# A recurrence joined over two batch elements, and one product in its plain form, in a DeltaNet and MLP-mixer kernel

## The chip, the core and the metric

The kernel runs on one core of a Trainium2 chip. The metric is the device time of one execution in microseconds (us), as the median of several runs of the same program. A core has five engines that run side by side, each with its own instruction stream: TensorE (PE in the profile) multiplies matrices into the accumulator memory PSUM, VectorE (DVE) and ScalarE (ACT) work elementwise and empty PSUM, GpSimd (POOL) works elementwise in SBUF, and SyncE (SP) issues the DMAs of this kernel. Engines wait for one another by semaphores.

## The reference

Four batch elements, eight heads, 768 rows in sequence, head dimension 48. A recurrence runs along the rows for each head, and its output is the input of a token and channel mixer:

```python
k_n = k / (np.linalg.norm(k, axis=-1, keepdims=True) + 1e-06)
state = np.zeros((B, H, D, D), dtype=np.float32)
for t in range(S):
    kt, vt, bt = (k_n[:, :, t], v[:, :, t], beta[:, :, t, None])
    y[:, :, t] = np.einsum('bhd,bhde->bhe', q[:, :, t], state)
    v_old = np.einsum('bhde,bhd->bhe', state, kt)
    state = state + bt[:, :, :, None] * np.einsum('bhd,bhe->bhde', kt, vt - v_old)
...
x = y.transpose(0, 2, 1, 3).reshape(B, S, H * D)      # 4 x 768 x 384
h = np.maximum(x.transpose(0, 2, 1) @ w_tok1, 0.0) @ w_tok2   # 768 -> 256 -> 768
u = x + h.transpose(0, 2, 1)
return u + np.maximum(u @ w_ch1, 0.0) @ w_ch2         # 384 -> 1536 -> 384
```

## The kernel before, in words

**Tiling of the recurrence.** The 768 rows of an element are cut into 6 *units* of 128 rows (24 units in all), and each unit into 2 chunks of 64 rows. A chunk is one *step* of the recurrence: 12 steps per element, 48 in all, one element after the other. The eight heads stand as 4 pairs; the two heads of a pair sit in the two halves of the 128 partitions, so that a matmul of one head uses a 64-row or 48-row part of TensorE's array.

**What a unit needs before its steps.** Job k loads k and q, p prepares them (norms, scaling, transposes), c and d form the products of the rows of a chunk among themselves (p_g, L453). A triangular matrix per chunk is inverted: t takes its parts out, i inverts several units at a time on VectorE (a *round*; the last two rounds hold units 18 to 21 and 22 to 23) after a passage through device memory (n_dram, then w_dram), f brings the parts back (gm<-w_dram), and h or j joins them with small matmuls (p_z, p_x). Job v loads v for a unit by four DMAs (L413) and scales it on POOL (L426) into a tile v_st, of which there are two buffers.

**One step** (recur, job r) is a chain through three engines:
- p_k: 8 matmuls of the state s_t with k (L862); then VectorE subtracts v, giving rest (L869)
- p_y and p_w: 16 matmuls of the state with q (L882) and of the inverse with rest (L886); then ACT copies p_w to w_t (L892)
- p_s and p_y: 16 matmuls of w_t (L900, L901); then VectorE subtracts p_s from the state (L909), and ACT puts p_y into xb by two instructions (L914). xb is the element's 768 x 384 array, the mixer's input.

**The mixer** of an element (job m) starts when its 12 steps are done. It multiplies xb with w_tok1 (p, L1060) and that with w_tok2 (p_h, L1073) and adds the result to xb (L1077). Then for three *pairs* of 128-row blocks: six transposes per pair (p_ut, L1083, copied to u_t at L1087), the first product with w_ch1 and a relu, and the second product with w_ch2 (p_o, L1162), added to xb (L1091) and stored (L1094). The second product always uses a form with 7 smaller products. The first has two forms, chosen by the constant FAST: elements below FAST (only element 0 here) take the plain one, p_c (L1140, relu at L1149); the others take a form with 15 smaller products, p_r (L1032), which needs sums of the input blocks (forms, L1001, on VectorE), sums of the weights (job s), and additions of its results (L1041 copies on ACT, L1044 additions on VectorE, relu at L1048). The buffer for weight sums, lent, first holds k and q of early units. Three PSUM banks serve the mixer, two the recurrence, two the preparation.

**What sets the order.** Every job is a Python generator that issues some instructions between two yields. A string `order` written out in the program says which job makes its next steps (`r24*5` is five pieces of step 24), so the interleaving on every engine is fixed by hand, with no scheduler. All DMAs stand in one queue on SP in the order of the string, and each also waits for the one eight before it. Elements' recurrence steps stand between the matmuls of the mixer of the element before. Element 3's mixer has nothing beside it.

Each fp32 matmul appears in the trace as two records, so that `x8` in the order of instructions is x16 in the trace.

## Time and profile before

| what | value |
|---|---|
| median of the runs | 639.9 us (639.62 to 640.89) |
| span of the profiled execution | 636.9 us |
| TensorE busy | 608.5 us (96%) |
| VectorE busy | 447.9 us (70%) |
| ScalarE busy | 268.0 us (42%) |
| GpSimd busy | 107.2 us (17%) |
| mean granted clock of TensorE | 0.976 |

The span runs from the first to the last instruction of one profiled execution. The time of a run also holds what lies around the span; by the median that is 3.0 us. Busy time is the union of an engine's instructions. Rows of the profile read: line and engine, operation, output<-inputs with shapes, count, busy time and mean duration in ns, then the engine's idle time just before these instructions and the instruction that ended it.

### The profile page before, as it was taken

How to read it: one execution, taken by the hardware profiler on the slowest of the kernel's cores; microseconds unless marked ns; L12 is line 12 of the kernel's file. 1: busy time of each engine (PE TensorE's matmuls, PEld its weight loads, DVE VectorE, ACT ScalarE, POOL GpSimd, SP SyncE). 2: the span in 40 equal slices, each digit the busy share in tenths (PEclk: the TensorE clock that was granted, in tenths of full speed). 3: DMA queues.
4: the chain of work that ended last, by engine and by line, in shares of the span. 5: the costliest groups of instructions: out<-in, count | busy, mean ns of one | idle time of the engine just before them, and what ended most of it. 6: DMA issues, size and time to landing. Idle time of an engine off the chain costs nothing.

```text
span 636.9 us, 21542 instructions
## 1 busy us (share of the span) xinstructions
PE 608.5 (96%) x9132; PEld 531.5 (83%) x9132; DVE 447.9 (70%) x1132; ACT 268.0 (42%) x693; POOL 107.2 (17%) x146
## 2 busy tenths in 40 slices
PE   8488988899999999999999999999999999999997
PEld 5367877668898988859889999769999987999997
DVE  4987876967999658988969987776728253373643
ACT  7758785447523342215624323325334130232240
POOL 2348354235210211111111001000010000000000
PEclk9978796999999999999999999999999999999999
DMA  9686666666543355344454223202020000000000
GB/s 201 127 148 151 153 142 153 162 135 162 110 113 89 71 116 101 76 109 79 90 103 95 43 82 58 48 5 42 5 53 2 27 2 0 26 1 26 2 26 26
DMA packets 135776, 50.27 MB, mean 79 GB/s; under 512 B 114656, under 2 KB 130144, under 8 KB 135680
## 3 DMA queue, kind: packets, MB, share of 16 engines
q1 hardware_dynamic: 135680, 48.89, 35.2%
q8 instruction: 72, 1.18, 0.8%
q14 instruction: 24, 0.20, 0.1%
HBM read 39.42 MB, written 9.44 MB: 77 GB/s over the span
## 4 chain that ended last, share of the span: by engine, by line
PE 82%; DVE 7%; ACT 4%; DMA 3%; issue 2%; POOL 1%; SPq 1%; ACTq 0%; DVEq 0%; POOLq 0%
PE p_o L1162 26%; PE p_r L1032 20%; PE p_c L1140 8%; PE p_h L1073 5%; PE p L1060 4%; PE p_k L862 3%; PE p_g L453 3%; PE p_y L882 3%; PE p_s L900 3%; PE p_w L886 1%; DVE sub L681 1%; DVE x L686 1%; PE p_y L901 1%; PE p_ut L1083 1%; PE p_z L785 1%
## 5 line engine op out<-in xcount | busy, mean ns | idle before, releaser
L1162 PE MATMUL p_o<-wc,r 128*128 128x192 f32 x720 | 126.1, 329 | 0.6 <-ACT u_t L1087 0.6
L1162 PEld LDWEIGHTS p_o<-wc,r 128*128 128x128 f32 x720 | 116.8, 190 | 2.7 <-ACT u_t L1087 1.1
L1044 DVE TENSOR_TENSOR r<-r,p_r 128x512 f32<-128x512 f32 x90 | 59.8, 684 | 38.1 <-PE p_r L1032 34.3
L1091 DVE TENSOR_TENSOR xb<-xb,p_o 128x192 f32<-128x192 f32 x84 | 29.3, 350 | 57.8 <-PE p_o L1162 57.3
L1041 ACT COPY r<-p_r 128x512 f32<-128x512 f32 x54 | 31.3, 585 | 85.7 <-PE p_r L1032 76.1
L686 DVE TENSOR_TENSOR x<-x,sub 128x84 f32<-128x84 f32 (+24 forms) x178 | 59.4, 334 | 6.1
L681 DVE TENSOR_TENSOR sub<-x 128x84 f32<-128x84 f32 (+24 forms) x178 | 58.0, 326 | 6.8 <-DMA x<-n_dram 2.3
L1162 PE MATMUL p_o<-wc,s 128*128 128x192 f32 x288 | 51.5, 331 | 0.3 <-DVE xb L1091 0.3
L1140 PE MATMUL p_c<-u_t,wc 128*128 128x256 f32 x216 | 51.0, 386 | 0.2 <-ACT u_t L1087 0.2
L1162 PEld LDWEIGHTS p_o<-wc,s 128*128 128x128 f32 x288 | 46.7, 190 | 1.4 <-DVE xb L1091 0.6
L1048 ACT ACTIVATE r<-r 128x512 f32<-128x512 f32 x54 | 34.0, 631 | 26.7 <-DVE r L1044 26.2
L426 POOL TENSOR_TENSOR v_st<-v_st,nrm 128x384 f32<-128x384 f32 x24 | 20.1, 838 | 146.3 <-DMA v_st<-in_v_dram 109.3
L1140 PEld LDWEIGHTS p_c<-u_t,wc 128*128 128x128 f32 x216 | 39.7, 190 | 6.0 <-ACT u_t L1087 0.4
L516 POOL TENSOR_TENSOR mb<-mask_c,cs 128x512 f32<-128x512 f32 x20 | 21.2, 1062 | 138.9 <-DVE cs L494 138.6
L914 ACT ACTIVATE xb<-p_y 64x192 f32<-64x192 f32 x96 | 31.2, 325 | 23.6 <-PE p_y L901 12.2
L892 ACT COPY w_t<-p_w 128x192 f32<-128x192 f32 x48 | 15.2, 316 | 58.0 <-PE p_w L886 57.5
L1032 PE MATMUL p_r<-u_t,wc 128*128 128x128 f32 x288 | 38.7, 277 | 0.0
L453 PE MATMUL p_g<-kq 48*64 48x128 f32 (+1 forms) x704 | 33.6, 281 | 3.8 <-ACT kq L529 3.3
L1032 PE MATMUL p_r<-t_d,wc 128*128 128x128 f32 x288 | 37.3, 280 | 0.0
L1032 PEld LDWEIGHTS p_r<-u_t,wc 128*128 128x128 f32 x288 | 35.3, 192 | 0.4
L1060 PE MATMUL p<-xb,w 128*128 128x384 f32 x96 | 34.9, 511 | 0.0
L1032 PEld LDWEIGHTS p_r<-t_d,wc 128*128 128x128 f32 x288 | 34.0, 192 | 0.8
(184 smaller groups left out, 1212.2 us busy)
## 6 DMA issues: line engine op xcount, KB each, us to landing
d<-in_moe_w_ch_dram SPq DMA_DIRECT2D x24, 384.0 KB, 3.5
v_st<-in_v_dram SPq DMA_DIRECT2D x96, 48.0 KB, 2.7
out_dram<-xb SPq DMA_DIRECT2D x23, 192.0 KB, 1.9
kst<-in_k_dram SPq DMA_DIRECT2D x64, 48.0 KB, 2.9
n_dram<-gm SPq DMA_DIRECT2D x72, 32.0 KB, 2.4
pads<-in_k_dram SPq DMA_DIRECT2D x24, 96.0 KB, 2.9
pads<-in_q_dram SPq DMA_DIRECT2D x24, 96.0 KB, 2.9
gm<-w_dram SPq DMA_DIRECT2D x72, 32.0 KB, 2.1
```

The source lines that it names most:

```text
L453: nc.tensor.matmul(p_g[PAR[i ^ cc], p], kqt[f, p, cc, 0], kqt[f, p, cc])
L681: nc.vector.tensor_tensor(out=tmp, in0=y[:, :, 0:s, s : s + 1].to_broadcast([n, k, s, w]), in1=y[:, :, s : s + 1, s + 1 : m].to_broadcast( ...
L686: nc.vector.tensor_tensor(out=y[:, :, 0:s, s + 1 : m], in0=y[:, :, 0:s, s + 1 : m], in1=tmp, op=ALU.add,)
L914: nc.scalar.mul(y[:, :, D * i : D * i + D], p_y[PAR[1 - i]], 1.0 if c else -1.0)
L1032: nc.tensor.matmul(p[:, i], pieces[i // width][:, at : at + 128], f[f"u{n}"], start=first and i == 0, stop=True, skip_group_check=True,)
L1041: nc.scalar.copy(o, p)
L1044: nc.vector.tensor_tensor(out=o, in0=o, in1=p, op=ALU.add if sign > 0 else ALU.subtract)
L1048: nc.scalar.activation(o, o, ACTF.Relu)
L1060: nc.tensor.matmul(p_1[dh], piece_of(w1, c, 0)[:, dh * 128 : (dh + 1) * 128], xb[:, c], start=(c == 0), stop=(c == NCH - 1),)
L1073: nc.tensor.matmul(p_h, piece_of(w2, j, c * 128)[:, c * 128 : (c + 1) * 128], r1[j], start=(j == 0), stop=(j == NDH - 1),)
L1140: nc.tensor.matmul(p_c[:, k], piece_of(wc1, cb, f * 128)[:, f * 128 : (f + 1) * 128], u_t[:, cb], start=(cb == 0), stop=(cb == NCB - 1),)
L1162: nc.tensor.matmul(p, a[:, m], wc2[:, m, j], start=(start and i == 0), stop=(i == NM - 1), skip_group_check=True,)
```

## The change

**One joint recurrence for elements 2 and 3.** Units 12 to 23 are numbered anew: even ones are chunks of element 2, odd ones the same chunks of element 3 (where). Steps 24 to 35 are 12 joint steps of 16 heads (recur_pair) in place of 24 steps of 8. Rest and w_t become one tile of double width, rw_t, the two buffers of the state become the halves of ss_t, for elements 2 and 3, and the norms stand in one tile. v is loaded per joint step, again by four DMAs and one scaling on POOL, into a tile of the same size as before.

**Element 3's rows pass through device memory.** Element 2's xb is filled as before. Element 3's rows of a step go into a spare part of the tile pads (side, the part that held the padded rows of early units), are stored to x_dram by one DMA of 96 KB per step (12 stores in all), and fetched into xb by 6 DMAs of 192 KB (fetch_last, job l) during element 2's mixer.

**Element 1's first product plain**: FAST goes from 1 to 2, so p_r and its forms are used for elements 2 and 3 only. The weight sums are now made just ahead of element 2's mixer.

**A new order** from the token `r9*2 i2 h5` on: the end of all recurrence, which stood in element 2's mixer, now stands in element 1's and at the very start of element 2's.

```diff
-    nrms = tiles("nrm", [128, NP, 2], NV + 2)
+    nrm_t = const.tile([128, NV + 2, NP, 2], FP32, name="nrm")
+    nrms = [nrm_t[:, i] for i in range(NV + 2)]
...
-    rest_t = const.tile([128, NP, D], FP32, name="rest")
-    w_t = const.tile([128, NP, D], FP32, name="w_t")
-    s_t = tiles("s_t", [128, NP, D], 2)
+    rw_t = const.tile([128, 2, NP, D], FP32, name="rw_t")
+    rest_t, w_t = rw_t[:, 0], rw_t[:, 1]
+    ss_t = const.tile([128, 2, NP, D], FP32, name="ss_t")
+    s_t = [ss_t[:, i] for i in range(2)]
...
-    FAST = 1
+    FAST = 2
...
+    JU = 2 * NCH
+    def where(u):
+        if u < JU:
+            return divmod(u, NCH)
+        c, e = divmod(u - JU, 2)
+        return 2 + e, c
...
+    def load_v_pair(t):
+        c, cc = divmod(t, 2)
+        us = [JU + 2 * c, JU + 2 * c + 1]
+        vsts["pair", t] = v_st = loads.tile([128, 2, NP, D], FP32, name="v_st")
+        for e, u in enumerate(us):
+            rows = heads_of(v, u)
+            for par in range(2):
+                nc.sync.dma_start(out=v_st[PAR[par ^ cc], e], in_=rows[par, cc])
+                yield
...
+    def recur_pair(c):
...
+        heads = [
+            (e, p, i, PAR[i ^ cc], PAR[1 - i])
+            for e in range(2) for p in range(NP) for i in range(2)
+        ]
...
+            for n, (e, p, i, r, _) in enumerate(heads):
+                f = FEATS[i]
+                nc.tensor.matmul(p_k[r, e, p], ops[e][1][f, p, cc, 0], ss_t[f, e, p])
...
+            nc.vector.tensor_tensor(out=rest, in0=p_k, in1=vsts["pair", c], op=ALU.subtract)
...
+        nc.scalar.copy(rw_t, p_w)
...
+                nc.vector.tensor_tensor(out=ss_t, in0=ss_t, in1=p_s, op=ALU.subtract)
...
+        nc.sync.dma_start(
+            out=x_dram[C * c : C * c + C].rearrange("s (i n) -> s i n", i=2),
+            in_=side[rows],
+        )
...
+    def fetch_last():
+        xbs[3] = mlp_pool.tile([128, NCH, DM], FP32, name="xb", tag="xb")
+        for c in range(NCH):
+            assert kept_out.issuperset((2 * c, 2 * c + 1))
+            nc.sync.dma_start(
+                out=xbs[3][:, c], in_=x_dram[c * 128 : (c + 1) * 128, :]
+            )
...
-    for t in range(B * NQ):
+    for t in range(B * NQ // 2):
         jobs[f"r{t}"] = recur(t)
+        if t < NQ:
+            jobs[f"r{B * NQ // 2 + t}"] = recur_pair(t)
+    jobs["l"] = fetch_last()
...
-    r46*4 m2*2 v23*2 r46 m2*9 r46*2 m2*2 r46*3 m2*7 r47*5 m2*6 r47 m2 r47
-    m2*2 r47 m2*6 r47 m3*6 m2*5 m3*6 m2*11 m3*3 m2 m3*159
+    v23*3 r35 m2 r32 r34*2 v23*2 r35*4 m2 r35*3 m2*91 r33 m2*21 r35 m2*5 r35 m2*8
+    l m2*19 l*4 m2*5 r34 m2*4 l m2*2 m3*12 m2*14 m3*3 m2 m3*159
```

What this does to the streams, at three places. First TensorE late in the recurrence. Before, in element 2's mixer, one of the last steps of the recurrence (p_k is its first product, kq the tile of k and q) stands between pieces of p_r:

```order
L862 MATMUL p_k<-s_t_112,kq_98 64x48 x8
L1032 MATMUL p_r<-u_t,lent 128x128 x2
L1032 MATMUL p_r<-u_t,wcx 128x128 x2
L1032 MATMUL p_r<-t_c,wc_125 128x128 x4
L1032 MATMUL p_r<-u_t,wc_125 128x128 x4
L882 MATMUL p_y<-s_t_112,kq_98 64x48
L886 MATMUL p_w<-rest,gm 64x48
```

After, joint step 31 stands between pieces of element 1's p_c:

```order
L1024 MATMUL p_y<-rw_t,gm 64x48
L1285 MATMUL p_c<-u_t,wc_116 128x256 x12
L985 MATMUL p_k<-ss_t,kq_99 64x48 x16
L1285 MATMUL p_c<-u_t,wc_116 128x256 x3
L1003 MATMUL p_y<-ss_t,kq_99 64x48
L1007 MATMUL p_w<-rw_t,gm 64x48
```

The burst of p_k has 16 matmuls in place of 8, and what stands before and behind it is p_c of element 1 and no longer p_r of element 2. Second, TensorE at a turn between two pairs of element 2's mixer, before (p_s and p_y belong to a recurrence step):

```order
L886 MATMUL p_w<-rest,gm 64x48
L1162 MATMUL p_o<-wc_126,r_6528 128x192 x6
L1083 MATMUL p_ut<-ident,xb 128x128 x6
L900 MATMUL p_s<-w_t,gm 64x48
L901 MATMUL p_y<-w_t,gm 64x48
```

and after:

```order
L1177 MATMUL p_r<-u_t,wc_116 128x128 x4
L1307 MATMUL p_o<-wc_117,r_6864 128x192 x6
L1228 MATMUL p_ut<-ident,xb 128x128 x6
L1307 MATMUL p_o_6960<-wc_117,r_6864 128x192 x6
L1307 MATMUL p_o<-wc_117,s_6952 128x192 x6
```

The recurrence between the transposes and the next product is gone from this turn. Third, SP around the last inverse round (n_dram, w_dram) and the loads of v, before:

```order
L1094 DMA out_dram<-xb 128x384 x2
L653 DMA gm<-w_dram 32x8x32 x4
L413 DMA v_st<-in_v_dram 64x4x48 x5
L705 DMA w_dram<-x 64x1024
L413 DMA v_st<-in_v_dram 64x4x48
L653 DMA gm<-w_dram 32x8x32 x3
L413 DMA v_st<-in_v_dram 64x4x48 x2
L653 DMA gm<-w_dram 32x8x32 x4
```

and after:

```order
L1239 DMA out_dram<-xb 128x384 x2
L1047 DMA x_dram<-pads 128x1x192
L454 DMA v_st<-in_v_dram 64x4x48 x4
L691 DMA gm<-w_dram 32x8x32 x4
L454 DMA v_st<-in_v_dram 64x4x48 x8
L743 DMA w_dram<-x 64x1024
L691 DMA gm<-w_dram 32x8x32 x8
L454 DMA v_st<-in_v_dram 64x4x48 x2
L1047 DMA x_dram<-pads 128x1x192
```

Stores of element 3's rows now stand among the loads of v, and the store of the last inverse has twelve loads of v ahead of it within this piece, in place of five.

More of the change, by code (lines that the diff above doesn't have):

```diff
@@ L375, in load_kq @@
     def load_kq(u):
-        b, c = divmod(u, NCH)
+        b, c = where(u)
         kst = kst_of[slot(u)]
@@ L418, in load_v @@
     def load_v(u):
+        if u >= JU:
+            yield from load_v_pair(u - JU)
+            return
         vsts[u] = v_st = loads.tile([128, NP, 2, D], FP32, name="v_st")
@@ L470, in prep @@
     def prep(u):
-        b, c = divmod(u, NCH)
+        b, c = where(u)
         kst = kst_of[slot(u)]
```

196 lines of the change are left out of this document (138 added, 58 removed).

## The prediction

> **What bounds the kernel now.** I read the page first, then stretches of it, then the order of TensorE's instructions in time.
>
> ```profile
> span 636.9 us, 21542 instructions
> ...
> PE 608.5 (96%) x9132; PEld 531.5 (83%) x9132; DVE 447.9 (70%) x1132; ACT 268.0 (42%) x693; POOL 107.2 (17%) x146
> ...
> PE   8488988899999999999999999999999999999997
> ...
> PE 82%; DVE 7%; ACT 4%; DMA 3%; issue 2%; POOL 1%; SPq 1%; ACTq 0%; DVEq 0%; POOLq 0%
> ```
>
> From the seventh slice on TensorE is busy without a break, and it carries 82% of the chain that ended last. The early 110 us are mixed. Two stretches make it sharper (columns: window, then busy time of each engine, granted clock, DMA share):
>
> ```profile
> 124.00:513.00 389.00, 386.54 (x6066) 338.79 (x6060) 291.76 (x747) 149.89 (x407) 52.31 (x71) 1.00 0.35 75
> 520.00:636.00 116.00, 113.08 (x759) 105.42 (x758) 55.25 (x129) 26.26 (x46) 0.00 (x0) 1.00 0.04 14
> ```
>
> From 124 to 513 us, where recurrence and mixers interleave, TensorE is idle for 2.5 us of 389, at full clock, while VectorE has 97 us to spare. So the time changes by what TensorE has to do, plus what it newly waits for. The rest comes from three questions: how long a large matmul takes in a stream, what a small group between large ones costs, and where the new order leaves nothing between dependent groups. The span is 636.9 us and the median of the runs 639.9, so 3.0 us lie around the span; I carry them over unchanged.
>
> **Element 1's first product, plain.** Each fp32 matmul is two records in the trace. The stretch of L1032 for one pair of row blocks, and a long run of L1140:
>
> ```profile
> 548.64:562.30 13.66, 13.66 (x120) 13.54 (x120) 1.00 0.04 16
> ```
>
> ```profile
> 192.10 2.11 PE L1140 MATMUL p_c<-u_t,wc 128*128 128x256 f32 x9
> 194.14 0.67 PE L862 MATMUL p_k<-s_t,kq 48*64 48x48 f32 x16
> 194.74 9.33 PE L1140 MATMUL p_c<-u_t,wc 128*128 128x256 f32 x42
> 203.90 0.33 PE L1162 MATMUL p_o<-wc,r 128*128 128x192 f32 x1
> ```
>
> The fast form costs 3 pairs x 13.66 = 41.0 us. The plain one has 216 records at (203.90 - 194.74)/42 = 0.218 us, 47.1 us. TensorE pays **+6.1 us**. The change also takes 30 additions (L1044), 18 copies (L1041), 18 activations (L1048) and 33 forms (L1001) away, and adds 18 activations of L1149:
>
> ```profile
> L1044 DVE TENSOR_TENSOR r<-r,p_r 128x512 f32<-128x512 f32 x90 | 59.8, 684 | 38.1 <-PE p_r L1032 34.3
> L1077 DVE TENSOR_TENSOR xb<-xb,p_h 128x384 f32<-128x384 f32 x24 | 13.0, 548 | 9.0 <-PE p_h L1073 8.9
> L869 DVE TENSOR_TENSOR rest<-p_k,v_st 128x192 f32<-128x192 f32 x44 | 15.5, 352 | 11.5 <-PE p_k L862 9.2 <-DMA gm<-w_dram 0.8 <-POOL v_st L426 0.7
> L909 DVE TENSOR_TENSOR s_t<-s_t,p_s 128x192 f32<-128x192 f32 x40 | 13.9, 348 | 14.5 <-PE p_y L901 14.4
> L892 ACT COPY w_t<-p_w 128x192 f32<-128x192 f32 x48 | 15.2, 316 | 58.0 <-PE p_w L886 57.5
> L1087 ACT COPY u_t<-p_ut 128x384 f32<-128x384 f32 x24 | 10.4, 482 | 44.7 <-PE p_ut L1083 44.7
> L839 ACT COPY gm<-p_x 32x128 f32<-32x128 f32 x20 | 5.1, 255 | 0.2
> L914 ACT ACTIVATE xb<-p_y 64x192 f32<-64x192 f32 x96 | 31.2, 325 | 23.6 <-PE p_y L901 12.2 <-PE p_s L900 5.1 <-DMA out_dram<-xb 2.9
> ```
>
> The additions alone are a third of L1044's 59.8 us. I cost this relief at nothing: it ran beside a TensorE that was full. It matters only because all recurrence must now end before element 2's mixer, so VectorE must do its part earlier.
>
> **The joint recurrence.** Its count of small matmuls is unchanged (736 + 736 + 352 in each program). What falls is the number of times TensorE leaves the large matmuls. In the rows above, p_c x9 would end its stream at 192.10 + 9 x 0.216 = 194.04; p_k starts 0.10 us later, holds 0.60 us, and the first p_c after it takes 0.10 us more than its stream: 0.80 us in all. The streaming part is eight groups of 0.06 us, as two rows four groups apart show:
>
> ```profile
> 227.85 0.22 PE L882 MATMUL p_y<-s_t,kq 48*64 48x48 f32 x1
> ...
> 228.09 0.22 PE L882 MATMUL p_y<-s_t,kq 48*64 48x48 f32 x1
> ```
>
> So 0.80 - 0.47 = 0.33 us is lost per excursion, whatever its length. In TensorE's order I count 106 excursions from full-array matmuls into 32- or 64-row ones and back before, and 70 after (36 steps of three bursts in place of 48, and bursts packed next to each other). The number of changes inside excursions is the same (125 and 126). 36 x 0.33 = **-11.9 us**. The lower bound is nothing at all, if a burst of sixteen groups lost what eight lose twice; I take the full price since excursions with three bursts (p_y, p_g, p_s) lose it once as well. What a wide step must empty between its bursts is longer than before: 548, 482 and 548 ns by the nearest rows of 128x384 (L1077 and L1087), against 352, 316 and 348. That is shorter than a burst of 0.94 us, and large matmuls stand between most bursts, so I take nothing for it; uncovered at all three hops of eleven steps it would be 33 x 0.5 = 17 us. The Trainium skill ("TensorEngine Tiling (Array Packing)", PSUM Bottleneck) says that packing the array speeds up the matmuls but not the emptying of PSUM, which may then be the limit; by that the change would end at those 17 us. The trace has 2.5 us of idle time with the narrow step, which speaks against it.
>
> **Gaps that go.** Before, one place packs two recurrence steps and waits for them:
>
> ```profile
> 318.06 0.67 PE L862 MATMUL p_k<-s_t,kq 48*64 48x48 f32 x16 [0.36 <-DVE s_t L909]
> ...
> 320.65 0.25 PE L900 MATMUL p_s<-w_t,gm 64*64 64x48 f32 x1 [0.46 <-ACT w_t L892]
> ...
> 321.89 1.10 PE L453 MATMUL p_g<-kq 48*64 48x128 f32 x32 [0.56 <-DVE kq L369]
> ```
>
> The new order has no such place there: **-1.4 us**.
>
> **Gaps that come.** First, element 2's mixer now runs without recurrence between its parts, as element 3's did:
>
> ```profile
> 564.26 0.82 PE L1083 MATMUL p_ut<-ident,xb 128*128 128x128 f32 x6
> 565.37 1.89 PE L1162 MATMUL p_o<-wc,r 128*128 128x192 f32 x10 [0.29 <-ACT u_t L1087]
> ```
>
> Six transposes stream for 0.65 us, so 0.46 us are lost at each of two turns. The first pair goes straight from p_ut to p_r (copy 482 ns, then two forms for the second product): 0.7 us; p to p_h without cover: 0.2 us. **+1.8 us**. Second, the start of element 1's recurrence:
>
> ```profile
> 138.60 0.43 DVE L755 STREAM_TRANSPOSE t<-gm 128x256 f32<-128x256 f32 x1
> ```
>
> ```profile
> 140.44 0.69 PE L793 MATMUL p_z<-t,gm 32*32 32x32 f32 x32
> ```
>
> It waits for the inverse's DMAs and is not moved, while TensorE reaches these matmuls, which need it, 1.7 us sooner, since eight records of p_c (8 x 0.218) no longer stand ahead. It can start them at 139.1 at the earliest: **+0.8 us**. Third, the last five joint steps. Their loads of v:
>
> ```profile
> L413 SPq DMA_DIRECT2D v_st<-in_v_dram x96: 595/614/2162, 9.2 to 472.1; - x96
> ...
> L426 POOL TENSOR_TENSOR v_st<-v_st,nrm x24: 827/829/987, 52.5 to 474.8; 128x384 f32<-128x384 f32 x24
> ...
> DMA to landing us min/median/max: 2.2/2.7/5.2
> ```
>
> Step 31's four loads stand on SP behind step 30's store to x_dram, which waits for four ACT copies: 0.3 + 4 x 0.325 + 0.6 + 3 x 0.61 + 2.7 + 0.83 + 0.55 + 0.3 = 8.4 us from step 30's last burst to the end of its own subtraction, against 7.8 us that TensorE has until then by its order, 30 records of p_c (6.5) and p_k with its excursion (0.94 + 0.33): 0.6 late. Before steps 32 and 34 the last four copies of a join (4 x 255 ns, after its p_x) end behind p_x with nothing between: 0.8 and 0.5. Step 33 has only p_z before it: 0.2. Together **+2.1 us**, from 0 (the copies overlap) to 6 (each load late). Behind that waiting SP stand the store of the inverse (w_dram) and the eight loads of its result for the last two units, which two more joins wait for.
>
> **Costed at nothing.** 12 stores and 6 loads through x_dram: 18 more DMAs.
>
> ```profile
> out_dram<-xb SPq DMA_DIRECT2D x23, 192.0 KB, 1.9
> ...
> out_dram<-xb SPq DMA_DIRECT2D x2, 96.0 KB, 1.6
> ```
>
> The loads are issued when element 2's second pair is stored, and 13.7 us of p_r follow before element 3's first product; the last store and its load, at 0.6 + 1.6 and 0.6 + 1.9 as in these rows, need about 5 us. Without that cover they cost those 5. Fewer ACT and VectorE instructions, merged tiles and the earlier weight sums lie beside a full TensorE.
>
> **The sum.** 6.1 - 11.9 - 1.4 + 1.8 + 0.8 + 2.1 = -2.5 us: span 634.4, time **637.4 us** (-0.4%).
>
> **The rivals.** *Clean gain*: the three new gaps are covered after all; 6.1 - 11.9 - 1.4 = -7.2, 632.7 us. For it: outside the rows quoted, 389 us passed with little idle time under the old order. Against: the turn at 564.26 is in the trace. *Waits eat it*: two or three more waits of 1 us, 638.6 to 641.2; SP is 0.6 us per DMA and has the same loads to issue some 50 us earlier. *The one-buffer drain* (slower): v of steps 31, 32, 33 and 35 goes into one of the two buffers, since the other holds step 34's, so each load waits for the step before's subtraction. A step then takes at least 4.5 (issue and landing) + 0.8 + 0.6 = 5.9 us, plus what stands ahead on SP. TensorE has 8 to 12 us of work per step by the order, so it decides once SP has more than 2 to 6 us ahead of a load; the eight loads of the inverse are 8 x 0.61 = 4.9. Two such steps, 3 us each, in place of the 2.1: 3.9 above the forecast, 641.3 us, and 644 with a third.
>
> ```profile
> PEclk9978796999999999999999999999999999999999
> ```
>
> ```profile
> 101.00:111.50 10.50, 9.69 (x190) 7.57 (x182) 6.33 (x23) 4.24 (x14) 3.23 (x5) 0.51 0.59 142
> ```
>
> *The clock* (slower): for 10.5 us from 101.0 TensorE was granted 0.51 of its clock, the last of such stretches in the early slices, and nothing like it follows. If a wait in the drain brought one back, some 10 us would take twice as long as the half of the work they hold: 5 us, 642.4. It decides only from a wait much longer than the 0.8 us I find. The Trainium skill ("TensorE: Matmul & The Clock Gate", HAM oscillation) says it bites from gaps in TensorE's work of about 3.4 us; by that, the waits of the forecast would not set it off, and only the one-buffer drain at its worst could. *It does not do what it says*: the count of excursions saves nothing because sixteen-group bursts cost what two bursts of eight did; -2.5 + 11.9 = +9.4, 649.3. Against it stands the streaming in the rows of 227.85, which has no cost that grows with a burst's length beyond 0.06 us a group. *The emptying of PSUM* (slower): the 17 us above, all uncovered, 637.4 + 16.5 = 653.9; it decides once a quarter of the hops stand bare.
>
> **How the numbers follow.** A kernel that repeats no closer than 639.62 to 640.89 can tell 0.2% (1.3 us) from no change, so 638.6 and 641.2 are the bounds. Forecast, 634.5 to 638.6: 0.40. Its lower end has the gaps that come at half their price, its upper end one more wait of a microsecond. Clean gain, 631.5 to 634.5: 0.18. Waits eat it, 638.6 to 641.2: 0.17. One-buffer drain, 641.2 to 644: 0.16. Clock: 0.06. No saving per excursion: 0.01. Emptying of PSUM: 0.02. So faster 0.40 + 0.18 = 0.58, the same 0.17, slower 0.16 + 0.06 + 0.01 + 0.02 = 0.25. For 8 in 10 I take 633.0 to 643.0: it leaves out half of the clean gain (0.09), the clock's worse end and some of the drain's tail (about 0.08), and the last two cases (0.03). The likeliest case's own range is 634.5 to 638.6.
>
> **What the profile after would show.** Right: p_r in 720 records and p_c in 432 (1080 and 216 before); TensorE idle by no more than 3 us between 124 us and the last joint step; bursts of 32 p_k records of about 1.1 us, with 0.1 us before and after; in element 2's mixer a 0.3 us wait at p_o after each p_ut; recurrence over some 110 us before the end; the subtraction of steps 31 to 34 waiting for v or for a join's copies, 0.2 to 0.8 us each; fetches from x_dram landing while p_r runs. A term is wrong if bursts of 32 take over 1.5 us (the excursions), if the wait before the subtraction in any late step is over 2 us and released by the loads of v (the drain), if element 3's first product waits for x_dram (5 us), or if a clock under 0.9 shows after 120 us. The whole is wrong if TensorE's idle time after 124 us grows by more than 9 us.

## The result and the profile after

The changed kernel takes 673.0 us (668.61 to 675.55) against 640.0 us for the kernel before on the same chip: a ratio of 1.051, with a 95% interval of 1.0465 to 1.055. It is 33 us slower, where 2.5 us of gain were forecast and 643.0 was the upper end of the range. The profiled execution has a span of 670.1 us, against 636.9 before.

The page of the changed kernel, the rows that answer those shown of before:

```profile
span 670.1 us, 21170 instructions
...
PE 618.9 (92%) x8988; PEld 534.8 (80%) x8988; DVE 426.0 (64%) x1047; ACT 256.8 (38%) x663; POOL 108.8 (16%) x146
...
PE   7488888989999888999989998999999999999998
...
PEclk9888996997999998999989999999999999999999
...
PE 58%; DVE 15%; SPq 9%; DMA 7%; ACT 7%; issue 4%; POOL 1%; DVEq 0%; ACTq 0%; POOLq 0%
PE p_o L1307 21%; PE p_r L1177 12%; PE p_c L1285 8%; DVE sub L719 4%; DVE x L724 4%; SPq L424 3%; PE p_h L1218 3%; PE p_g L491 3%; PE p L1205 2%; DMA d<-in_moe_w_ch_dram 1%; SPq L691 1%; PE p_k L985 1%; SPq L666 1%; DMA x<-n_dram 1%; SPq L371 1%
```

TensorE's row has eights in slices 9, 14 to 16, 21 and 25, where there were nines only; the clock, full from the eighth slice on before, falls again in the 10th, 16th and 21st (the stretches below). The share of TensorE in the chain fell from 82% to 58%. What took its place is VectorE (7% to 15%), SP (1% to 9%) and the DMAs (3% to 7%), and the last row names the work: L719 and L724 are the inverse on VectorE, L424 the load of k.

Stretches of the changed kernel (columns as before: window, busy time of TensorE, its weight loads, VectorE, ScalarE, GpSimd, granted clock, DMA share, GB/s):

```profile
124.00:470.00 346.00, 323.60 (x5428) 274.34 (x5420) 231.82 (x570) 117.24 (x340) 53.21 (x70) 0.97 0.37 84
151.60:158.40 6.80, 5.77 (x43) 4.79 (x44) 4.91 (x11) 3.90 (x11) 3.90 (x5) 0.50 0.97 245
233.50:236.90 3.40, 3.40 (x11) 3.40 (x12) 1.50 (x4) 2.13 (x8) 0.00 (x0) 0.50 0.43 106
260.80:264.20 3.40, 3.40 (x93) 3.33 (x94) 1.23 (x2) 0.00 (x0) 0.00 (x0) 0.50 0.12 20
346.10:352.90 6.80, 5.91 (x137) 5.49 (x138) 4.58 (x9) 1.76 (x5) 1.20 (x2) 0.50 0.33 57
470.00:670.00 200.00, 195.56 (x1339) 181.40 (x1337) 98.45 (x228) 51.54 (x90) 0.00 (x0) 1.00 0.06 20
```

The same window of the kernel before:

```profile
124.00:470.00 346.00, 343.64 (x5416) 298.03 (x5408) 272.50 (x701) 133.08 (x366) 49.71 (x67) 1.00 0.38 83
```

TensorE is idle for 22.4 us there, and was for 2.4. The four short rows are the stretches at half clock, which before had none after 124 us; they hold 18.5 us of work that would have taken half as long, so 9.2 us. These two, +20.0 and +9.2, make 29 of the 33 us. They leave no room for the 5.8 us (6.1 - 11.9) by which TensorE's own work was to fall; that comes back at the end. Behind 470 us TensorE is idle for 4.4 us, 2.7 of them after its last matmul; from the last step of the recurrence to that matmul it waits for 1.7 us, 0.9 more than before. VectorE and ScalarE are busy for less of the window than before, so over the window as a whole neither is full.

The longest waits of TensorE in that window (columns: in total, times, longest):

```profile
PE p_z L823 <- DVE t L793: 3.8, 3, 1.9
PE p_o L1307 <- ACT r L1294: 3.0, 1, 3.0
PE p_s L938 <- ACT rw_t L930: 2.9, 4, 1.2
PE p_o L1307 <- DVE xb L1236: 1.9, 2, 1.5
PE p_z L826 <- DMA gm<-w_dram: 1.9, 1, 1.9
PE p_c L1285 <- ACT r L1294: 1.4, 2, 0.7
PE p_g L491 <- DVE kq L380: 1.4, 1, 1.4
```

No row here is a joint step waiting for its own products; the first such row, p_w for the rest of its step, stands further down with 1.0 us in three waits. TensorE waits for preparation (t, kq, gm) and for ordinary work of the mixer (r, xb) and of element 1's steps (rw_t). The longest shows why the second kind is late. The timeline of SP, ScalarE and TensorE around 344 us (start, length, instruction; in brackets the idle time before it and what ended it):

```profile
327.94 3.01 SPq L371 DMA_DIRECT2D pads<-in_q_dram  x4
331.00 2.91 SPq L666 DMA_DIRECT2D n_dram<-gm  x4
334.01 4.14 SPq L454 DMA_DIRECT2D v_st<-in_v_dram  x5
338.25 1.97 SPq L371 DMA_DIRECT2D pads<-in_k_dram  x4
340.32 2.58 SPq L424 DMA_DIRECT2D kst<-in_k_dram  x4
...
339.84 0.60 ACT L1294 ACTIVATE r<-p_c 128x512 f32<-128x512 f32 x1 [3.22 <-PE p_c L1285]
344.77 0.52 ACT L519 ACTIVATE ksq<-kst 128x384 f32<-128x384 f32 x1 [4.33 <-DMA kst<-in_k_dram]
345.91 0.21 ACT L527 ACTIVATE nrm<-ksum 128x8 f32<-128x8 f32 x1 [0.62 <-DVE ksum L522]
346.15 0.30 ACT L528 ACTIVATE ksum<-nrm,eps 128x8 f32<-128x8 f32 x1
346.36 0.58 ACT L1294 ACTIVATE r<-p_c 128x512 f32<-128x512 f32 x1
...
336.94 5.45 PE L1285 MATMUL p_c<-u_t,wc 128*128 128x256 f32 x24
342.23 1.79 PE L1307 MATMUL p_o<-wc,r 128*128 128x192 f32 x10
346.99 1.01 PE L1307 MATMUL p_o<-wc,r 128*128 128x192 f32 x2 [2.97 <-ACT r L1294]
```

SP issues one DMA behind the other, so that the four loads of a unit's k stand at 340.3. ScalarE's next instruction is the square of that k (L519); it sits idle for 4.33 us until the data lands, and two norm steps that follow wait for VectorE. Behind them in ScalarE's queue stands the relu of the mixer (L1294), whose input p_c was finished by 342.4; TensorE goes idle at 344.02 and waits 2.97 us for it. The mixer was not slow; a late piece of preparation stood ahead of it. During this wait, at 346.1, the clock halves for 6.8 us.

### The profile page after: what moved, and what is told of

Read it like the earlier page. It is cut to its first block, busy times and chain, and to the rows that moved or that the text cites. A ratio compares the mean times of both kernels' runs of the same rounds, so it can differ in the third digit from the quotient of the medians.

```text
span 670.1 us, 21170 instructions
## 1 busy us (share of the span) xinstructions
PE 618.9 (92%) x8988; PEld 534.8 (80%) x8988; DVE 426.0 (64%) x1047; ACT 256.8 (38%) x663; POOL 108.8 (16%) x146
## 4 chain that ended last, share of the span: by engine, by line
PE 58%; DVE 15%; SPq 9%; DMA 7%; ACT 7%; issue 4%; POOL 1%; DVEq 0%; ACTq 0%; POOLq 0%
PE p_o L1307 21%; PE p_r L1177 12%; PE p_c L1285 8%; DVE sub L719 4%; DVE x L724 4%; SPq L424 3%; PE p_h L1218 3%; PE p_g L491 3%; PE p L1205 2%; DMA d<-in_moe_w_ch_dram 1%; SPq L691 1%; PE p_k L985 1%; SPq L666 1%; DMA x<-n_dram 1%; SPq L371 1%
## 5 line engine op out<-in xcount | busy, mean ns | idle before, releaser
L1285 PE MATMUL p_c<-u_t,wc 128*128 128x256 f32 x432 | 103.4, 392 | 1.6 <-ACT r L1294 1.4
L1285 PEld LDWEIGHTS p_c<-u_t,wc 128*128 128x128 f32 x432 | 81.4, 194 | 14.3 <-ACT r L1294 2.2
L719 DVE TENSOR_TENSOR sub<-x 128x84 f32<-128x84 f32 (+24 forms) x178 | 60.1, 338 | 16.3 <-DMA x<-n_dram 11.5
L1189 DVE TENSOR_TENSOR r<-r,p_r 128x512 f32<-128x512 f32 x60 | 40.2, 686 | 39.7 <-PE p_r L1177 39.6
L724 DVE TENSOR_TENSOR x<-x,sub 128x84 f32<-128x84 f32 (+24 forms) x178 | 61.1, 343 | 6.1
L1294 ACT ACTIVATE r<-p_c 128x512 f32<-128x512 f32 x36 | 21.4, 595 | 65.4 <-PE p_c L1285 65.3
L497 DVE TENSOR_TENSOR gm<-p_g,mb 128x512 f32<-128x512 f32 x44 | 29.0, 684 | 13.7 <-PE p_g L491 12.7
L491 PEld LDWEIGHTS p_g<-kq 48*64 48x64 f32 (+1 forms) x704 | 28.7, 148 | 7.7 <-ACT kq L567 4.3
L1218 PE MATMUL p_h<-r,w 128*128 128x384 f32 x96 | 32.8, 493 | 0.4 <-DVE xb L1222 0.4
L286 POOL TENSOR_TENSOR wc<-w_f,d 128x384 uint32<-128x384 uint32 x24 | 24.6, 1027 | 47.1 <-DVE w_f L282 14.5
L464 POOL TENSOR_TENSOR v_st<-v_st,nrm 128x384 f32<-128x384 f32 x12 | 10.7, 894 | 130.2 <-DMA v_st<-in_v_dram 90.6
L1218 PEld LDWEIGHTS p_h<-r,w 128*128 128x128 f32 x96 | 17.3, 189 | 14.7 <-ACT r L1213 3.7
L1193 ACT ACTIVATE r<-r 128x512 f32<-128x512 f32 x36 | 22.7, 631 | 15.4 <-DVE r L1189 15.0
```

Source lines behind the costliest of these rows:

```text
L286: nc.gpsimd.tensor_tensor(out=dst.bitcast(U32), in0=f, in1=lo, op=ALU.add)
L491: nc.tensor.matmul(p_g[PAR[i ^ cc], p], kqt[f, p, cc, 0], kqt[f, p, cc])
L497: nc.vector.tensor_tensor(out=blocks(gm_of(u))[:, :, cc, D:GW].rearrange("s p (two n) -> s p two n", two=2), in0=p_g, in1=made[u][:, :, cc ...
L719: nc.vector.tensor_tensor(out=tmp, in0=y[:, :, 0:s, s : s + 1].to_broadcast([n, k, s, w]), in1=y[:, :, s : s + 1, s + 1 : m].to_broadcast( ...
L724: nc.vector.tensor_tensor(out=y[:, :, 0:s, s + 1 : m], in0=y[:, :, 0:s, s + 1 : m], in1=tmp, op=ALU.add,)
L1189: nc.vector.tensor_tensor(out=o, in0=o, in1=p, op=ALU.add if sign > 0 else ALU.subtract)
```

## The experiments

Idle time and half clock of TensorE from 124 us on, for all kernels (idle: 346.0 us less TensorE's busy time in the window 124 to 470 us; half clock up to the last 5 us; ratio to the kernel before on the same chip, with its interval; for the kernel reordered behind 124 us the profiled execution took 670.0 us against a median of 663.2, so its idle time and half clock are rather too high):

| kernel | ratio | idle, us | half clock, us |
|---|---|---|---|
| before | 1 | 2.4 | 0 |
| after | 1.051 (1.047 to 1.055) | 22.4 | 20.5 |
| plain product alone | 1.019 (1.012 to 1.025) | 6.8 | 3.4 |
| loads on GpSimd's queue | 1.048 (1.043 to 1.052) | 19.2 | 20.5 |
| waits filled | 1.048 (1.043 to 1.052) | 16.0 | 6.8 |
| element 1 with 15 products | 1.127 (1.123 to 1.132) | 58.4 | 54.6 |
| 88 loads left out | 1.033 (1.028 to 1.039) | 15.0 | 10.2 |
| half the late inverses left out | 1.038 (1.033 to 1.042) | 16.9 | 10.2 |
| both left out | 1.015 (1.011 to 1.020) | 8.3 | 6.8 |
| before, half the late inverses | 1.000 (0.998 to 1.003) | 3.0 | 0 |
| reordered | 1.045 (1.043 to 1.047) | 12.2 | 3.4 |
| rows not stored | 1.048 (1.045 to 1.051) | 19.5 | 20.5 |
| reordered behind 124 us | 1.039 (1.034 to 1.044) | 14.8 | 13.7 |
| that, and both left out | 1.031 (1.026 to 1.035) | 11.1 | 6.8 |

### One part alone: element 1's plain product in the old kernel

```diff
+            if b == 1:
+                at = {2 * (g * 15 // 12): g for g in range(2 * NM)}
...
+                        for cb in range(NCB):
+                            nc.tensor.matmul(
+                                p_c[:, k],
+                                piece_of(wc1, cb, f * 128)[:, f * 128 : (f + 1) * 128],
+                                u_t[:, cb], start=(cb == 0), stop=(cb == NCB - 1),
+                            )
...
-            if b >= FAST:
+            elif b >= FAST:
```

> The kernel before with element 1's first product in its plain form and nothing else: the same 48 steps, the same order, the p_c matmuls spread over the places where the 15 products stood, and the 16 weight sums moved behind element 1's last first product (they overwrite its weights). Theory (the new order and the joint steps made the 33 us, not the product): 640.0 + 6.1 for the matmuls, and up to 4 us for the weight sums, which now stand in 15 us of work on VectorE: 646 to 650. Rival (the plain product itself makes TensorE wait, since its 18 activations and the banks of p_c stand closer): 655 or more, with TensorE's idle time between 124 and 513 us up from 2.5 to over 10.

Measured 649.9 us against 636.8 on the same chip: 13 us more (8 to 16 by the interval), where the theory had 6 to 10. The rival's 655 us and its 10 us of idle time did not come. TensorE's own work is some 7 us of it, by an estimate: busy time less half of the work at half clock is 602.5 us here and 595.5 in the kernel before. The rest is mostly idle time (6.8 us against 2.4 in the window), and 3.4 us stand at half clock. So this part of the change, too, disturbed work that was said to be covered.

### The loads of the padded rows on another queue

```diff
-                nc.sync.dma_start(
+                nc.gpsimd.dma_start(
```

> The changed kernel with the 96 loads of k and q rows of units 12 to 23 (L371, 0.43 to 0.6 us each on SP, some 50 us of its time) issued from GpSimd's queue instead of SP's. Theory (SP's queue is the limit from 140 to 460 us: it issues back to back and loads come late): TensorE's idle time of 23 us falls by 8 or more and with it the stretches at half clock, 655 to 663. Rival one (the order puts the consumers too close behind their loads, whatever SP has to do): the loads are no earlier, 671 to 675. Rival two (GpSimd's queue blocks its own elementwise work): 680 or more, with new waits for GpSimd.

Measured 667.5 us, in none of the three ranges, and no gain that the intervals show. The waiting for free buffers moved to the other queue. GpSimd's own waits in this run:

```profile
POOL v_st L464 <- DMA v_st<-in_v_dram: 75.8, 9, 13.1
...
POOL pads L371 <- DVE sub L719: 15.8, 2, 10.4
POOL pads L371 <- DVE rw_t L907: 14.6, 1, 14.6
...
POOL pads L371 <- DVE kq L380: 9.8, 3, 7.4
```

A load of padded rows may not start before its buffer is free, and now GpSimd stands still for that in place of SP, 40 us in the three rows, with the scaling of v and the masks behind it. The first row is not new: in the changed kernel GpSimd waits 90.6 us for the loads of v. The Trainium skill ("Perfetto Trace Analysis", DMA Optimizations) says that spreading DMAs over the engines that can issue them may help where generating their descriptors is the limit. This run shows no such gain. That the place in a queue which executes in order is what counts, and not the issuing alone, fits these rows but is not shown by itself, and it stays open what an otherwise empty queue would do.

### The clock alone: filling the waits

```diff
-    j8 r13*2 p12*4 r13*2 w25*3 k12*2 v7*4 m0*2 w21*3 k12 p12*3 w20*2 w31 w20*2 f9
+    r13*2 d11 w30*3 v7 f7 m0 p12 j8 w25*3 r13 z*2 j8 r13 z r13 p12*4 r13*2 w25*3
```

The lines are one of the places where the order was written anew. Each z is one large independent matmul that nobody reads; ten of them more than in the changed kernel stand at six of its longest waits.

> The changed kernel with ten spare matmuls (p_warm, about 1.06 us each) put just ahead of the six longest waits of TensorE behind which the granted clock falls to one half (at 148, 151, 230, 242, 259 and 344 us); they compute nothing that is used. Theory (the four stretches at half clock, 20.5 us in all, come from 1.3 to 3 us of waiting within some 3.4 us, and cost about 9 us beside the waits): the clock stays at 1.00 after 124 us and the time falls by 6 to 9, 664 to 667. Rival one (the lost clock is hidden behind late loads, which set the pace): 671 to 675 with the clock at 1.00. Rival two (the clock falls for another reason than idle time): the stretches stay, 673 to 680.

Measured 668.6 us. The half clock after 124 us fell from 20.5 to 6.8 us, at two new places, which by the work in it is worth 6 us, but the time fell by about 2. With most of the half clock gone the kernel hardly noticed. One reason is that, while preparation is late, a faster TensorE only arrives sooner at the next wait. Another is not ruled out: the ten matmuls are some 9 us of work (0.43 us a record in a row), and they took only 6.4 us out of the idle time. The 9.2 us of the clock are in any case no item that fillers give back.

### More work for the same queues: element 1 with 15 products again

```diff
-    FAST = 2
+    FAST = 1
```

> The changed kernel with element 1's first product back in its 15-product form (the weight sums made before it, its pieces spread over the places of the plain ones). The prediction's term says 673.0 - 6.1 = 667. Theory (between 140 and 460 us VectorE and SP, not TensorE, set the pace, so 30 more additions of 684 ns, 33 forms and 16 earlier weight sums, some 30 us on VectorE, cannot be hidden there): slower by 15 to 40, 688 to 713.

Measured 718.5 us, more than either theory said. The longest waits of TensorE:

```profile
PE p_r L1177 <- DVE r L1189: 16.3, 3, 12.5
PE p_o L1307 <- ACT r L1193: 6.5, 2, 4.9
```

With the additions and copies of the 15 products back on VectorE and ScalarE beside the joint steps' preparation, TensorE waits up to 12.5 us at one place. The relief that the plain product gives these two engines, costed at nothing, is worth more here, under this order of the pieces, than the 6 us it costs on TensorE.

### Preparation taken away

The first edit leaves out 88 of the 96 loads of padded rows (L371), the second every second step of the inverse's late rounds.

```diff
+                if u == 12:
                   nc.sync.dma_start(
```

> The changed kernel without 88 of the 96 loads of k and q rows (L371): units 13 to 23 compute on the rows of unit 12, which leaves out that part of the input and nothing else. SP has some 44 us less to issue between 124 and 400 us and no elementwise queue has more. Theory (the work that prepares 12 units, SP's issues first, sets the pace from 140 to 460 us): the waits of TensorE fall by half and with them the half clock, 653 to 661. Rival (the order puts matmuls too close behind their producers, and SP's load does not matter): 669 or more.

```diff
+            if rnd >= 3 and s % 2 == 0:
+                yield
+                continue
```

> The changed kernel with every second step of the inverse left out in the rounds of units 10 to 23 (its output is no inverse then): 150 instructions on VectorE of some 340 ns, about 50 us, are gone, none of TensorE's, SP's or ACT's. Theory: VectorE's part of the same chain is as tight, 648 to 658. Rival (SP alone is the limit, VectorE has a third of its time free and it costs nothing): 668 or more.

> Both of these together, in the changed kernel. Theory: with the preparation out of the way TensorE sets the pace again, and the prediction's sum comes out: no half clock after 124 us, TensorE idle by less than 8 us there, 634 to 644. Rival (joint steps or the plain product have a cost of their own on TensorE that the sum lacks, such as the emptying of PSUM): 650 or more, with the waits at the joint steps' own hand-overs.

> The kernel before with the same steps of the inverse left out: the control of e6. Theory (in the old order TensorE sets the pace and the preparation has time to spare): faster by 2 to 6 only, 634 to 638. Rival (the inverse costs as much in either order): faster by 15 or more, 620 to 625.

Measured: 660.3 us without the loads, 664.1 with half the late inverses, 649.9 without either, and 639.8 for the kernel before with half the late inverses, against 639.0 for the kernel before. This is the comparison that decides. The same omission that gains 8 us in the new program (1.051 to 1.038) gains nothing (1.000, 0.998 to 1.003) in the old one, where 2 to 6 us had been expected: there the inverse was covered, here it is not. The loads were not left out of the old program; with 2.4 us of idle time and no half clock after 124 us, waiting could not have given back more than that there. The time without the loads is within its expectation, though TensorE's waits fell by a third and not by half; with half the inverses it is a miss, and the edit took 120 instructions and 40 us off VectorE's busy time, not 150 and 50. And leaving out both, which touches no matmul of the recurrence or the mixers, brings back 23 of the 33 us. The second row of the chain, by line, without the loads, with half the inverses, and without both:

```profile
PE p_o L1308 18%; PE p_r L1178 13%; DVE x L725 7%; PE p_c L1286 7%; DVE sub L720 6%; PE p_h L1219 3%; DMA x<-n_dram 2%; PE p_g L492 2%; SPq L692 2%; PE p L1206 2%; SPq L667 2%; DMA d<-in_moe_w_ch_dram 1%; DMA gm<-w_dram 1%; SPq L455 1%; DVE kq L381 1%
```

```profile
PE p_o L1310 21%; PE p_r L1180 12%; PE p_c L1288 9%; PE p L1208 4%; PE p_h L1221 4%; SPq L424 3%; PE p_g L491 2%; DMA gm<-w_dram 2%; DMA d<-in_moe_w_ch_dram 2%; DVE x L727 2%; DVE sub L722 2%; SPq L371 1%; PE p_k L988 1%; SPq L691 1%; DMA pads<-in_q_dram 1%
```

```profile
PE p_o L1311 22%; PE p_r L1181 13%; PE p_c L1289 12%; PE p L1209 4%; PE p_h L1222 4%; DVE x L728 2%; DVE sub L723 2%; PE p_g L492 2%; SPq L692 2%; DMA d<-in_moe_w_ch_dram 2%; PE p_k L989 1%; DMA gm<-w_dram 1%; DMA pads<-in_k_dram 1%; SPq L425 1%; PE p_s L942 1%
```

In the changed kernel the inverse (sub and x) and the load of k held 4%, 4% and 3% of the chain. Take the loads away, and the inverse grows to 7% and 6%; halve the inverse, and it falls to 2% and 2% while the loads stay. This reads as two limits, one behind the other, and would explain why half the inverses alone gained less than the theory expected; that the two together gain more (23 us) than their sum (11 and 8) is within the intervals. The run with both gone was still 6 us over the upper end of its expectation and stands at the rival's 650. 8.3 us of idle time are left, 3.6 of them in two waits at 147 and 151 us, before the joint steps; the first brings the one stretch of half clock. The rival's sign, waits at the joint steps' own hand-overs, did not come, but its other half, work on TensorE that the sum lacks, is borne out in the last part.

The preparation's own clock tells the same without leaving anything out. The store of an inverse's result (w_dram) ends a round of it. Its row in the trace of before and of after (count, duration in ns, first and last start in us):

```profile
L705 SPq DMA_DIRECT2D w_dram<-x x5: 332/345/494, 131.8 to 437.1; - x5
```

```profile
L743 SPq DMA_DIRECT2D w_dram<-x x5: 326/350/490, 132.3 to 439.2; - x5
```

| kernel | last inverse stored | last step of the recurrence (its first p_w) | between |
|---|---|---|---|
| before | 437.1 | 512.9 | 75.8 |
| before, half the late inverses | 435.4 | 513.6 | 78.2 |
| after | 439.2 | 465.5 | 26.3 |
| waits filled | 436.5 | 462.6 | 26.1 |
| loads left out | 423.3 | 452.0 | 28.7 |
| half the late inverses | 428.4 | 455.5 | 27.1 |
| both left out | 413.6 | 441.1 | 27.5 |

The changed kernel ends the recurrence 47 us sooner, but the preparation that feeds it ends no sooner than under the old order (439.2 against 437.1). Before, 75.8 us lay between the two and hid it. In the changed program the recurrence ends 26 to 29 us behind the last inverse, whatever is left out, and when an omission makes the inverse earlier the end comes with it. A fixed order would keep such a distance by itself, so the distance does not say which holds up which; the omissions do.

### Element 3's rows

```diff
-        nc.sync.dma_start(
-            out=x_dram[C * c : C * c + C].rearrange("s (i n) -> s i n", i=2),
-            in_=side[rows],
-        )
...
-                out=xbs[3][:, c], in_=x_dram[c * 128 : (c + 1) * 128, :]
+                out=xbs[3][:, c], in_=v[3].rearrange("h s d -> (h s d)").rearrange("(s n) -> s n", n=DM)[c * 128 : (c + 1) * 128, :]
```

> The changed kernel without its 12 stores to x_dram; the 6 loads stay and fetch other rows, of v, into element 3's xb (element 3's output is therefore not what the reference gives, and nothing else in time changes). Theory (the passage of element 3's rows costs nothing): 668 to 674 us beside a kernel before at 637 to 640, ratio 1.045 to 1.055. Rival (the stores wait on SP for the ACT copies, 29.5 us in three waits with the longest 16.1, and the loads of the next joint steps' preparation stand behind them): 5 to 10 us less, 660 to 667 us, ratio 1.035 to 1.043.

Measured 669.3 us, ratio 1.048, as the theory had it and the changed kernel's within the intervals. The stores to device memory cost nothing that these show, though in the changed kernel they do wait on SP. The six loads stay in this run and are not tested by it.

### The order alone

```diff
-    f13*3 j11 r20*2 j12*2 r20*2 t14 r20*2 k16*7 m0 j12 m0 r21 s*2 r21*2 c15 r21 c15*3
+    k15 r19 j11 j10 f12 j11 r19 r20 k15 f12 p15*2 f12 m0 r20 p15 k16 r20*2 k16 p15
```

> The changed kernel with every instruction kept and only the order written out anew, from the middle of element 0's steps on: pieces of preparation, their loads and stores, the inverse's steps and the mixers' pieces stand at other places, so that the loads are issued earlier and no piece stands ahead of one that is wanted sooner. Theory (the preparation for the joint steps sets the pace only because of where it stands in SP's, ACT's and VectorE's queues): TensorE's idle time between 124 and 470 us falls from 22 us to under 12, no stretch at half clock is left after 124 us (9 us of work), so the span falls from 670 to 648 to 654 and the time to 649 to 656, with the order's other program, the one before, still 10 to 16 us faster. Rival one (twelve units' preparation is too much for the queues in 320 us, wherever it stands): waits move but stay, 663 us or more. Rival two (TensorE's own work fell by the 5.8 us of the forecast, and waits and clock are all that hid it): with under 12 us of idle time left the time would be 642 us or less.

Measured 667.6 us, in rival one's range. From 124 us on it nearly did what the theory asked: idle 12.2 us, one stretch of half clock of 3.4 us. That is 10.2 us less waiting and some 7.5 us less lost to the clock, but the span fell by 5.1 us only. Part of the rest was lost ahead of 124 us:

```profile
100.00:124.00 24.00, 15.61 (x321) 11.73 (x315) 16.42 (x44) 8.67 (x26) 9.81 (x14) 0.57 0.63 143
124.00:470.00 346.00, 333.76 (x5598) 275.94 (x5597) 236.36 (x585) 123.89 (x354) 54.66 (x71) 1.00 0.39 87
```

The first row is the stretch ahead: 8.4 us of idle time and a clock of 0.57 (3.2 us and 0.72 in the changed kernel). Over the whole of the first 124 us that comes to 4.2 us more idle time and no more work at half clock. The larger part, some 8 us, is TensorE's own work by the estimate used above (606.8 us against 598.5). The next expectation puts the whole loss on the early stretch, which is too much. The order of the first 124 us was put back, with the rest rearranged in the same way, and both omissions were added in a second kernel:

> As the reordered kernel before it, but the order is that of the changed kernel up to 124 us, and only what comes behind is written anew. In the first reordered run TensorE's idle time from 124 to 470 us fell from 22.4 to 12.2 us, as theory asked, but a wait of 5.8 us at 108 us and 20.5 us at half clock up to 123 us were new; step 12 began at 152.7 us and not 143.2, and with that it lost what it had won. Theory (the preparation's place in the queues is what costs; the early loss was a fault of that order): step 12 begins at 143 to 145 us again, idle time from 124 to 470 us stays at 8 to 13 us with at most one stretch of 3.4 us at half clock, and the time is 667.6 less 8 to 11: 654 to 661 us, 12 to 19 us under the changed kernel. Rival (whatever is won behind 124 us comes back as other waits): 664 us or more. By the forecast's saving on TensorE, with so little idle time left, it would be 648 us or less.

> The same order, and 88 of the 96 loads of the padded rows and every second step of the late inverses are left out (as in the run with both left out; the output is not the reference's). Almost nothing is then left for TensorE to wait for, so the time shows what the change does to TensorE's own work. Theory (its work stays about as it was: the run with both left out had a span of 645.7 us, 5.9 us more idle time from 124 us on than the kernel before and 3.4 us lost at half clock, which leaves 636.4): 638 to 644 us, ratio 0.999 to 1.008, with under 5 us of idle time between 124 and 470 us. By the forecast (5.8 us less work, 1.4 us of turns): 636 us or less, ratio 0.995 or less. Rival (the joint steps' own hand-overs wait even with everything ready): 646 us or more.

Measured 663.2 us for the order and 657.8 us with both left out. Both miss. The order alone is worth some 7 us (1.051 to 1.039), less than expected. Idle time in the profiled execution falls by a third and no more, so the rest of the preparation's lateness is not a matter of place, at least not of one that these orders found. The second miss has a reason that can be counted: by TensorE's order the changed kernel leaves the large matmuls 70 times, the reordered one 86 times, since its pieces are cut finer. From 124 us on, the time of these groups without their waits (from the end of the large record ahead to the second large record behind, less the large records' own time) is 97.5 us in 49 groups where both were left out in the change's own order, and 105.0 us in 65 groups here. Sixteen more groups took 7.5 us more, of the 10.5 us by which the span is longer (656.2 against 645.7); 2.8 us are idle time in the window. With the preparation taken away the new places gain nothing, and the cut-up stream loses. The waits at the joint steps' own hand-overs, the rival's reason, come to about 1 us. None of the versions beats the kernel before.

## Why the prediction was wrong

**The step that failed** is the preparation that must be ready sooner and has no price in the sum. The prediction names it, "so VectorE must do its part earlier", and then costs it at nothing: fewer instructions on ScalarE and VectorE and earlier weight sums "lie beside a full TensorE". Its ground was that 389 us had passed with little idle time under the old order. But that idle time was small because the old order consumed the preparation late: its last inverse was stored 75.8 us before the last step. The forecast's span of 634.4 would put the last step near 430 us (465.5 less the 35.7 us by which the span exceeds it), some 83 us sooner than before and ahead of a last inverse that was stored at 437.1 in the profile of before. Nothing in the sum makes the preparation end sooner, so that row spoke against it, and it was not read. In place of nothing, the runs showed 20.0 us more idle time and 9.2 us lost to half clock after 124 us, and 23 of the 33 us came back when preparation was left out. A stall did not move; cover was spent.

Two readings were off as well. TensorE's row of before has eights up to the eighth slice, so it is busy without a break from the ninth on and not the seventh. And among the signs the recurrence was to end some 110 us before the end; it does so 204.6 us before, against 124.0 in the kernel before. By that sign the end of the recurrence would hardly have moved towards its producers, so the size of the move was not worked out.

**The small terms of waiting** were about right. The last five joint steps, costed at 2.1 us, lie in the stretch from 415 to 470 us, which has 1.6 us of idle time. At the start of element 1's recurrence, costed at 0.8 us, 0.2 came at its first joins, and 1.9 at the next unit's, at 148.7. Behind the recurrence 0.9 us more waiting came, where 1.8 had been put for waits and turns together, and the wait at the turn is there:

```profile
497.73 2.22 PE L1307 MATMUL p_o<-wc,r 128*128 128x192 f32 x12 [0.30 <-ACT u_t L1232]
```

The 12 stores to x_dram cost nothing that the intervals show. For the 6 loads there is only the profile of the changed kernel: no wait of TensorE behind 124 us names them.

**Excursions** are the second term that failed: right in kind, too large by about a third. A burst of 32 records holds TensorE for little longer than the stream asks:

```profile
283.54 1.14 PE L985 MATMUL p_k<-ss_t,kq 48*64 48x48 f32 x32
```

With its two changes that makes 1.26 us against 2 x 0.80, so 0.34 us saved, as said. But summed over all groups from 124 us on, without waits and with 4304 small records in either run, the kernel before has 105.8 us in 85 groups and the run with both left out 97.5 us in 49: 8.3 us less, some 9 if the half clock of that run is taken off, where 36 x 0.33 = 11.9 was forecast. The single bursts do give 0.33 to 0.34 us, so other groups give less; which of them was not tested.

**The plain product**: 720 records of p_r and 432 of p_c came as said. The lone edit cost 13 us, waits and clock included; the estimate of some 7 us on TensorE does not speak against the 6.1. That the relief of VectorE and ScalarE is worth nothing was wrong: without it the changed kernel took 718.5 us.

**The rivals.** *Waits eat it* had the mechanism, SP with the same loads to issue some 50 us earlier, but priced it as two or three waits of 1 us. *The clock* was priced as one stretch of 10 us that costs 5 us; four came, of 3.4 to 6.8 us, 9.2 us together, from waits of 1.4 to 3.0 us. The emptying of PSUM did not occur, with 1.0 us of waits for a joint step's own rest, and neither did the one-buffer drain: VectorE waits at most 0.9 us ahead of the subtraction in the last five steps. Two of the signs that were named for a wrong forecast came: idle time after 124 us grew by more than 9 us, and the clock fell after 120 us.

**What stays open**: with both omissions the span is 8.8 us over that of the kernel before. TensorE is idle for 10.0 us more, 5.9 of them between 124 and 470 us, and loses 2.9 us less to half clock, since the early stretches are shorter in this run; that leaves its own work up by about 2 us. This rests on the estimate that work at half clock takes twice as long: 595.5 us before, 597.2 with both left out, 598.5 in the changed kernel, and 594.5 in the other run of the old order. The forecast had the own work fall by 5.8 us. The plain product at some 7 us and the excursions at 9 would still have it fall by 2; where the other 4 us are was not followed up. So even with preparation for free the change would hardly have gained the forecast 2.5 us; whether it would have gained anything is within what these runs can tell.

## What to carry to other kernels

An engine that is full says nothing on how much slack its feeders have: before moving consumers forward, read when the last producer finishes and how long its result lies unused, and subtract the move from that. Where queues run in order, one late piece of preparation delays every finished piece behind it on that engine, so a late load shows up as waits for work that has nothing to do with it. A control in the old program, the same omission there and here, separates hidden work from limiting work at the price of one run.

## What the runs showed of the hardware

The clock can fall after little idle time. In the changed kernel all four drops follow a stretch of about 3.4 us in which TensorE was busy for only 0.39 to 0.51 of the time, where the longest gaps were 1.9, 1.7, 1.4 and 3.0 us (2.1 us of the last one before the drop), and each lasts 3.4 or 6.8 us. The Trainium skill ("TensorE: Matmul & The Clock Gate", HAM oscillation) gives as the rule to leave no idle gaps over some 3.4 us; the window's length agrees with these multiples of 3.41 us, but by that rule none of the four would have come. The measurement decides: here 1.7 to 2.1 us of idle time within 3.4 us were enough. That is no threshold. Without the 88 loads the clock fell at 435.5 us behind a stretch that was busy for 0.68 of the time, with one gap of 1.1 us; in the changed kernel it stayed at 1.00 behind the stretch from 407.5 to 410.9 us, which was busy for 0.54. What tells the two apart was not tested.

Issuing the padded rows' loads takes longer on GpSimd's queue than on SP's, 550 against 431 ns (the second of the three durations, minimum, median and maximum):

```profile
L371 POOL DMA_DIRECT2D pads<-in_q_dram x47: 550/550/576, 153.8 to 383.8; - x47
```

```profile
L371 SPq DMA_DIRECT2D pads<-in_q_dram x45: 317/431/1702, 151.8 to 391.6; - x45
```
